# A gated attention unit feeding a long convolution: four late stores on another engine, idle products in the tail, and a plan with twenty sets of weights

## The chip, the cores and the metric

The kernel runs on one core of one Trainium2 chip. The core has a matrix engine (TensorE, PE in the profile, with PEld for its weight loads), VectorE (DVE), ScalarE (ACT), GpSimd (POOL), SyncE (SP), which here only issues transfers, and 16 DMA engines that carry all transfers. The engines run their own instruction streams in order and wait for each other on semaphores. The metric is device time in microseconds. The kernel before takes 990.45 us, the median of 3 runs (990.18 to 990.82).

## The reference

```python
def _attn_ref(u, v, z):                      # u, v: (8, 3136, 256), z: (8, 3136, 64)
    scores = (1.0 / S) * np.matmul(z, z.transpose(0, 2, 1))
    attn = np.maximum(scores, 0.0) ** 2
    out = np.matmul(attn, v)
    return (u * out).astype(np.float32)

def _moe_ref(x, w_proj, filter_fft, w_out):  # x is the output above
    proj = x @ w_proj                        # 256 -> 768
    x1, x2, x3 = proj[..., :D], proj[..., D:2 * D], proj[..., 2 * D:]
    X2 = np.fft.rfft(x2, n=S, axis=1)
    H = np.fft.rfft(filter_fft, n=S, axis=0)[None, :, :]
    x2_conv = np.fft.irfft(X2 * H, n=S, axis=1)
    y = x1 * x2_conv * x3
    return (y @ w_out).astype(np.float32)
```

There are 8 batches with a sequence of S = 3136 = 64 x 49 rows. Inputs and output are float32.

## The kernel before

**Stages of a batch.** The sequence of a batch is cut into seven chunks of columns (512, 512, 512, 512, 512, 256 and 320). For each chunk, score products (`ps_s<-zT_t`) go through ScalarE's relu (L1792) into `R_t`, are squared by VectorE (L1801) or ScalarE (L1799) into `A_t`, and are weighted with v (`ps_o_t<-A_t,v_t`). Scores are symmetric, so some blocks are turned by DMA (`M_t`, `M2e_t`, `M2o_t`) and used a second time. When a chunk's weighted sum is complete, VectorE multiplies it by u into `xT_t` (L1843); the projection products with `wp` give the two gates (`gate_t`, L1162) and the convolution's input `x_t`, which a first Fourier step (`ps_s<-x_t,T`) turns into `s_t`. That is stored to DRAM (`spec<-s_t`, L966).

When all seven chunks are stored, the batch's spectrum follows: it is loaded back in four loads (`spec_in_t<-spec`, L996; in the last batch the third and the fourth load go to `M_t` and `M2e_t`), and eight groups each take a forward product (weights `S`), two evictions, the filter's multiplication on VectorE (L1250), an inverse product (weights `TZ`), and two evictions; the results are stored to DRAM (`spec<-gs_t` and other homes, L1295) and loaded again by chunk (L1008: `conv_in_t`, and in the last batch `A_t` and `v_t`). The end of a chunk is a last Fourier step (`ps_s<-T,conv_in_t`), the gate's multiplication (`yT_t`, L1344), the output product (`wo,yT_t`), its eviction (L556 on ScalarE or L560 on VectorE, 512 columns each) and the store (`out_dram`, L1404).

**Order.** Batches overlap: one batch's projections, spectrum and chunk ends run between the scores of the next. The order is not the compiler's. A planner (class `Plan`) is run while the program is built. Each piece of work is a `Task` with a cost, dependencies and buffers; the planner keeps a clock for each engine, and picks for TensorE from the queues S (scores), Q (spectrum products), W (weighting), FA (projections and the first Fourier step), FB and FZ (other and put-off work: FZ has the last chunk ends of the batch before the last, and the last batch's gates). `pick_pe` chooses by seven numbers, a `Rule`; an eighth, `give`, is used by `pick`, which lets a copy go to ScalarE or VectorE. `rule(t)` takes the rule of the planned time t from the list `RULES`, one for each stretch of `STEP` = 50 us; in the kernel before the list has a single entry, so it holds throughout. What the planner settles is an order on each engine; the chip keeps the order and not the planned times.

**The tail.** After the last batch's last weighting nothing is left but work that depends on it: the last chunk's projection, the last store of `s_t`, the spectrum, the seven chunk ends (`add_end` with `FINAL` = (0, 2, 4, 6, 1, 3, 5) as their order), and the put-off chunk ends of the batch before, whose stores POOL issues. A chunk end's output of the last batch is stored in two halves of 64 partitions: for the chunks 0, 2, 4, 6, 1 and 3 POOL issues one half and SP the other; for chunk 5 ScalarE and SP do.

**The end.** After its last instruction each engine drains and meets the others at a barrier (L1932 in the profile), where SP also waits for the outstanding transfers.

Of the kernel before, what the change touches and what calls it, by code (L numbers as in the profile page):

```python
# [12 lines left out]
P = 128  # L13
# [17 lines left out]
LATE_F = 6.0  # L31
LATE_OUT = 1.5
LATE_POOL = 0.0
AFTER = (1, 3, 5, 6)
FINAL = (0, 2, 4, 6, 1, 3, 5)
ZP, ZL = 0, 0.0
# [1 line left out]
REACH = 2  # L38
Rule = namedtuple("Rule", "backlog ample stay first lead pace full give")
STEP = 50.0  # L40
RULES = [Rule(1.25, 5.0, 0.05, 0.5, 1, 0.5, 3.0, 1.0)]
SHARE = {0: 1, 2: 3}

ISSUED = "issued"
# [15 lines left out]
    return sum(n / 2400 + 0.003 for n in ns)  # L60


DMA_GO, DMA_DONE = {"SP": 0.3, "POOL": 2.0}, 0.9
LAT = {"PE": 0.22, "ACT": 0.22, "DVE": 0.19, "POOL": 0.15, "SP": 0.0}


# [117 lines left out]
class Plan:  # L184
# [151 lines left out]
    def pick(self, e):  # L336
# [18 lines left out]
                best = (key, s, task)  # L355
        return best and (best[1], best[2], e)

    def go(self):
        while True:
            got = []  # L360
            x = self.pick_pe()
            if x:
                got.append((x[0], 0, x[1], "PE", x[2]))
            for i, e in enumerate(self.pend):
                x = self.pick(e)
                if x:
                    got.append((x[0], i + 1, x[1], e, None))
            if not got:
                break
            start, _, task, e, k = min(got, key=lambda g: g[:2])  # L370
            if k:
                self.queues[k].remove(task)
                half = k in ("S", "Q")
                if half != (self.mode == "S") and self.mode:
                    start += 0.096
                    self.quarters, self.quad_run, self.score_run = half and self.soon, 0, 0
                self.score_run += k == "S"
                if k == "Q":
# [15 lines left out]
def kernel(  # L394
# [10 lines left out]
    nc = tc.nc  # L405
# [25 lines left out]
    plan = Plan()  # L431
# [270 lines left out]
    plan.free["POOL"] = 12.0  # L702
    plan.free["SP"] = 3.0
    plan.free["DVE"] = 1.5


    def after(task, at):
# [607 lines left out]
    def add_end(b, lasts, gtasks, cs, kind="FB", src=c_p, dsts=(o_p,), late=0, behind=(), then=(), split=False, mids=(y_p,)):  # L1315
        for at, c in enumerate(cs):
# [89 lines left out]
            if split and c == cs[-1]:  # L1406

                def both_queues(nt=nt, store=store):
                    store(0, nt, (0,))
                    store(0, nt, (1,), nc.scalar)  # L1410

                s_ = on("SP", both_queues, 0.6, [*oe, *behind], prio=1, moves=0.45 * nt)
            elif b == B - 2:
                s_ = on(
                    "POOL", lambda nt=nt, store=store: store(0, nt, by=nc.gpsimd), 1.2, [*oe, *behind],
                    moves=0.45 * nt, late=LATE_POOL,
                )
            elif split:
                s_ = on("POOL", lambda nt=nt, store=store: store(0, nt, (0,), nc.gpsimd), 0.6, [*oe, *behind], moves=0.22 * nt)
                s_ = on("SP", lambda nt=nt, store=store: store(0, nt, (1,)), 0.8, [*oe, *behind], prio=1, moves=0.22 * nt)  # L1420
            else:
                s_ = on("SP", lambda nt=nt, store=store: store(0, nt), 1.3, [*oe, *behind], prio=1, moves=0.45 * nt, late=LATE_OUT * (dst is o_p))
# [514 lines left out]
```

## Time and profile before

| | |
|---|---|
| median of 3 runs | 990.45 us |
| the profiled execution's own time | 992.91 us |
| its span, first to last instruction | 991.0 us |
| PE / DVE / ACT / POOL busy in the span | 946.0 / 831.3 / 857.8 / 207.7 us |
| granted TensorE clock, mean | 0.989 |
| DMA, mean over the span | 172 GB/s |

How to read the rows that are quoted below. A timeline row gives start, duration, engine, line, operation, output and inputs by the program's names, and a count; square brackets hold the idle time before it and what ended that. SPq, ACTq and POOLq are the sequencers of these engines, where the issue of a transfer stands. A row of the chain of waits gives start, duration and what the chain went through: an engine's line, a transfer (DMA), or "issue" where the profile shows no cause. A row of a stretch gives its bounds, then for PE, PEld, DVE, ACT and POOL the busy time and in brackets the number of instructions, then the granted clock, the mean busy share of the 16 DMA engines, and GB/s.

### The profile page before, as it was taken

The numbers are of one execution on the slowest core, as the hardware profiler recorded it, in microseconds if no ns is written. First come the engines' busy times: TensorE is split into PE (matmuls) and PEld (weight loads), VectorE is DVE, ScalarE is ACT, GpSimd is POOL, SyncE is SP. The second block draws the span as 40 slices with busy tenths as digits, with TensorE's granted clock in tenths as the row PEclk, the third lists the DMA queues.
The fourth block names the chain that finished last, engine by engine and source line by source line (L and its number), as shares of the span: only waits on it lengthen the run. The fifth ranks groups of instructions, "written<-read, shape, count | busy, mean of one in ns | idle before, by whom it ended". The sixth has DMA issues, their size and how long they took to land.

```text
span 991.0 us, 19581 instructions
## 1 busy us (share of the span) xinstructions
PE 946.0 (95%) x6774; PEld 471.2 (48%) x6878; DVE 831.3 (84%) x1461; ACT 857.8 (87%) x1192; POOL 207.7 (21%) x430
## 2 busy tenths in 40 slices
PE   6999999999999999999999999999999999999984
PEld 2344544455544545445454444445454455544643
DVE  7966798999798887988789887898879988799874
ACT  5988888899888997899988989799988899998673
POOL 5142311212021312113111320122202230001031
PEclk9999999999999999999999999999999999999978
DMA  9799879979899679997799788997889968985676
GB/s 159 144 174 168 134 151 169 177 131 168 190 206 179 127 150 220 195 174 149 148 219 200 152 137 161 218 200 136 162 171 220 193 126 175 186 219 108 167 214 199
DMA packets 332355, 170.32 MB, mean 172 GB/s; under 512 B 242582, under 2 KB 307926, under 8 KB 332256
## 3 DMA queue, kind: packets, MB, share of 16 engines
q1 hardware_dynamic: 302720, 132.82, 63.3%
q0 software_dynamic: 29456, 36.12, 23.6%
q8 instruction: 54, 0.88, 0.4%
q14 instruction: 45, 0.37, 0.1%
q10 hardware_dynamic: 80, 0.13, 0.0%
HBM read 90.26 MB, written 53.35 MB: 145 GB/s over the span
## 4 chain that ended last, share of the span: by engine, by line
PE 77%; DVE 7%; issue 6%; ACT 4%; DMA 4%; SPq 1%; POOL 1%; POOLq 0%; ACTq 0%; DVEq 0%
PE ps_o_t L523 44%; PE ps_s L523 32%; DVE A_t L1801 4%; ACT R_t L1792 3%; DVE xT_t L1843 1%; DMA uT_t<-un_t 1%; DMA spec<-s_t 1%; DMA ost_t<-in_z_dram 1%; DMA M_t<-spec 1%; ACT s_t L556 1%; SPq L996 0%; DMA specf<-s_t 0%; DVE gs_t L560 0%; ACT gs_t L556 0%; DVE xh L1250 0%
## 5 line engine op out<-in xcount | busy, mean ns | idle before, releaser
L1792 ACT ACTIVATE R_t<-ps_s 128x1024 f32<-128x1024 f32 (+4 forms) x512 | 467.5, 963 | 83.0 <-PE ps_s L523 79.3
L523 PE MATMUL ps_o_t<-A_t,v_t 128*128 128x512 bf16 (+4 forms) x2006 | 447.2, 353 | 11.9 <-issue 5.2
L1801 DVE TENSOR_TENSOR A_t<-R_t 128x1024 bf16<-128x1024 f32 (+2 forms) x324 | 354.1, 1112 | 55.5 <-ACT R_t L1792 55.0
L523 PEld LDWEIGHTS <-v_t 128*128 128x128 bf16 (+1 forms) x2884 | 248.9, 98 | 260.6 <-issue 81.4
L1799 ACT ACTIVATE A_t<-R_t 128x1024 bf16<-128x1024 f32 (+3 forms) x172 | 175.0, 1026 | 1.2
L523 PE MATMUL ps_s<-zT_t 64*64 64x512 bf16 (+4 forms) x1526 | 173.5, 358 | 1.5 <-DVE zT_t L560 0.5
L606 POOL COPY tick<-xT_t 1x1 bf16<-1x1 bf16 x54 | 19.5, 362 | 695.9 <-DVE xT_t L1843 695.9
L523 PE MATMUL ps_s<-xT_t,wp 128*128 128x512 bf16 (+2 forms) x418 | 102.8, 352 | 4.5 <-ACT R_t L1792 2.3
L523 PEld LDWEIGHTS <-zT_t 64*64 64x64 bf16 (+1 forms) x1559 | 52.1, 101 | 107.8 <-issue 93.2
L556 ACT ACTIVATE x_t<-ps_s 128x512 bf16<-128x512 f32 (+2 forms) x170 | 89.7, 583 | 11.8 <-PE ps_s L523 10.1
L1843 DVE SCALAR_TENSOR_TENSOR xT_t<-ps_o_t,uT_t 128x256 bf16<-128x256 f32 (+2 forms) x224 | 76.0, 382 | 8.7 <-PE ps_o_t L523 5.6
L523 PE MATMUL ps_o_t<-M_t,v_t 128*128 128x512 bf16 (+2 forms) x352 | 82.3, 353 | 0.1
L1250 DVE TENSOR_TENSOR xh<-xh,H 128x1024 bf16<-128x1024 bf16 x120 | 82.0, 684 | 0.2
L1162 DVE TENSOR_TENSOR gate_t<-ps_s,x_t 128x256 bf16<-128x256 f32 (+2 forms) x212 | 70.3, 383 | 14.0 <-PE ps_s L523 12.9
L1344 DVE TENSOR_TENSOR yT_t<-ps_s,gate_t 128x512 bf16<-128x512 f32 (+2 forms) x100 | 59.0, 619 | 11.1 <-PE ps_s L523 10.3
L523 PEld LDWEIGHTS <-wp 128*128 128x128 bf16 x448 | 42.9, 98 | 47.1 <-issue 11.0
L597 POOL DMA_DIRECT2D un_t<-in_u_dram x112 | 59.8, 556 | 6.4 <-issue 4.5
L616 POOL DMA_DIRECT2D v_t<-in_v_dram x112 | 59.4, 555 | 3.8 <-PE ps_s L523 1.7
L560 DVE CAST xh<-ps_s 128x512 bf16<-128x512 f32 x61 | 41.1, 688 | 22.6 <-PE ps_s L523 21.3
L523 PE MATMUL ps_s<-wp,xT_t 128*128 128x256 bf16 x396 | 56.3, 273 | 0.1
L523 PE MATMUL ps_s<-wo,yT_t 128*128 128x256 bf16 (+1 forms) x350 | 51.7, 274 | 1.7 <-DVE yT_t L1344 1.7
L556 ACT ACTIVATE s_t<-ps_s 128x512 bf16<-128x512 f32 (+1 forms) x82 | 46.8, 589 | 2.1 <-PE ps_s L523 1.1
(160 smaller groups left out, 828.4 us busy)
## 6 DMA issues: line engine op xcount, KB each, us to landing
out_dram<-ost_t SPq DMA_DIRECT2D x60, 256.0 KB
spec<-s_t SPq DMA_DIRECT2D x96, 128.0 KB
spec_in_t<-spec SPq DMA_DIRECT2D x60, 192.0 KB
spec<-gs_t SPq DMA_DIRECT2D x59, 192.0 KB
v_t<-in_v_dram POOLq DMA_DIRECT2D x80, 128.0 KB, 4.4
un_t<-in_u_dram POOLq DMA_DIRECT2D x80, 128.0 KB, 5.1
conv_in_t<-spec SPq DMA_DIRECT2D x33, 256.0 KB
out_dram<-ost_t SPq DMA_DIRECT2D x18, 128.0 KB
```

The source lines that it names most:

```text
L523: wrote(nc.tensor.matmul(o, *args, **kw), o)
L556: got = nc.scalar.activation(out_, in_, AF.Copy)
L560: got = nc.vector.tensor_copy(out_, in_)
L597: nc.gpsimd.dma_start(out=t[ds(j * N1, N1), lo - t0 : hi - t0, :], in_=x[:, n2 : n2 + hi - lo, :])
L616: nc.gpsimd.dma_start(out=t[ds(j * N1, N1), ds(v_at(a), (b - a) * D)], in_=r[:, n2 + a - lo : n2 + b - lo, :].rearrange("p t d -> p (t d)"),)
L1162: got = nc.vector.tensor_tensor(g[:, ::-1] if h == 0 else g, p, x, ALU.mult)
L1250: nc.vector.tensor_tensor(x[:, 1 - i], x[:, 0], h, ALU.mult)
L1344: got = nc.vector.tensor_tensor(yb["y"][:, dh, 0:w], p, gates[b, c, dh][:, 0:w], ALU.mult)
L1792: has_read(nc.scalar.activation(blocks(box["R"], n, cw)[:rows], p, AF.Relu), p)
L1799: nc.scalar.activation(a, r, AF.Square)
L1801: nc.vector.tensor_tensor(a, r, r, ALU.mult)
L1843: nc.vector.scalar_tensor_tensor(x, f, inv_s2, ut, ALU.mult, ALU.mult)
```

## The change

There are three parts. First, the list of rules has twenty entries. Those of the stretches from planned time 0 to 600 equal the old rule, but for one number (`pace` 0.55) in the seventh; of the eight from 600 on, four differ in `give` alone (0 in place of 1.0) and four in two to six numbers. Second, the planner gets a function `fill`: where neither scores nor weighting are left, and the next task that is picked would start at least 0.25 us (`SPARE`) after an extra product of 512 columns could have ended, such a product is put there: `ident` times a broadcast of itself, into a free bank that nobody reads. Third, in the last batch the half that POOL stored is issued by ScalarE from the third chunk in the order on (chunks 4, 6, 1 and 3); chunks 0 and 2 remain with POOL.

In the program as built, TensorE's order is the same for the first 8,155 of its 13,758 instructions (its weight loads included), and 2,502 of the rest stand in blocks that differ. 19 idle products are added, all behind the last weighting. Beside these, only the form of some products differs: among the scores of 512 columns, 20 products with weights of 64 columns are fewer and 10 with weights of 128 columns are more, since `plan.quarters` decides whether a product is issued whole or in two halves.

```diff
+SPARE = 0.25
-RULES = [Rule(1.25, 5.0, 0.05, 0.5, 1, 0.5, 3.0, 1.0)]
+RULES = [
+    Rule(1.25, 5.0, 0.05, 0.5, 1, 0.5, 3.0, 1.0),
...
+    Rule(1.25, 5.0, 0.05, 0.5, 1, 0.55, 3.0, 1.0),
...
+    Rule(1.25, 5.0, 0.05, 0.5, 1, 0.5, 3.0, 1.0),
+    Rule(1.5, 6.0, 0.15, 1, 1, 0.4, 4.0, 1.0),
+    Rule(1.25, 5.0, 0.05, 0.5, 1, 0.5, 3.0, 0),
+    Rule(2, 5.0, 0.3, 0.5, 1, 0.5, 3.0, 1.0),
+    Rule(1.25, 5.0, 0.1, 0.5, 1, 0.5, 3.5, 1.0),
+    Rule(0.75, 5.0, 0.3, 0.5, 1, 0.5, 3.5, 0.5),
+    Rule(1.25, 5.0, 0.05, 0.5, 1, 0.5, 3.0, 0),
+    Rule(1.25, 5.0, 0.05, 0.5, 1, 0.5, 3.0, 0),
+    Rule(1.25, 5.0, 0.05, 0.5, 1, 0.5, 3.0, 0),
+]
-DMA_GO, DMA_DONE = {"SP": 0.3, "POOL": 2.0}, 0.9
+DMA_GO, DMA_DONE = {"SP": 0.3, "ACT": 0.5, "POOL": 2.0}, 0.9
+    def fill(self, until):
+        if self.queues["S"] or self.queues["W"] or not any(self.queues.values()):
+            return False
+        half = 0.096 * (self.mode == "S")
+        start = self.free["PE"] + half
+        if until < start + c_pe(512) + half + SPARE or self.singles.when() > start:
+            return False
+        self.bank, self.got = self.singles, [(self.singles, self.singles.take(start))]
+        self.filler()
+        self.free["PE"] = start + c_pe(512)
+        self.singles[self.got[0][1]] = self.free["PE"]
+        self.mode, self.quarters = "W", False
+        return True
+
     def go(self):
...
             start, _, task, e, k = min(got, key=lambda g: g[:2])
+            if self.fill(start):
+                continue
...
+    plan.singles = one_slots
+    plan.filler = lambda: matmul(bank(), ident[:], ident[:].unsqueeze(1).to_broadcast([P, 4, P]), start=True, stop=True)
...
+            elif split and c in cs[:2]:
+                s_ = on("POOL", lambda nt=nt, store=store: store(0, nt, (0,), nc.gpsimd), 0.6, [*oe, *behind], moves=0.22 * nt)
+                s_ = on("SP", lambda nt=nt, store=store: store(0, nt, (1,)), 0.8, [*oe, *behind], prio=1, moves=0.22 * nt)
             elif split:
-                s_ = on("POOL", lambda nt=nt, store=store: store(0, nt, (0,), nc.gpsimd), 0.6, [*oe, *behind], moves=0.22 * nt)
+                s_ = on("ACT", lambda nt=nt, store=store: store(0, nt, (0,), nc.scalar), 0.55, [*oe, *behind], moves=0.22 * nt)
                 s_ = on("SP", lambda nt=nt, store=store: store(0, nt, (1,)), 0.8, [*oe, *behind], prio=1, moves=0.22 * nt)
```

More of the change, by code (lines that the diff above doesn't have):

```diff
@@ L40 @@
 STEP = 50.0
-RULES = [Rule(1.25, 5.0, 0.05, 0.5, 1, 0.5, 3.0, 1.0)]
+RULES = [
+    Rule(1.25, 5.0, 0.05, 0.5, 1, 0.5, 3.0, 1.0),
+    Rule(1.25, 5.0, 0.05, 0.5, 1, 0.5, 3.0, 1.0),
+    Rule(1.25, 5.0, 0.05, 0.5, 1, 0.5, 3.0, 1.0),
+    Rule(1.25, 5.0, 0.05, 0.5, 1, 0.5, 3.0, 1.0),
+    Rule(1.25, 5.0, 0.05, 0.5, 1, 0.5, 3.0, 1.0),
+    Rule(1.25, 5.0, 0.05, 0.5, 1, 0.5, 3.0, 1.0),
+    Rule(1.25, 5.0, 0.05, 0.5, 1, 0.55, 3.0, 1.0),
+    Rule(1.25, 5.0, 0.05, 0.5, 1, 0.5, 3.0, 1.0),
+    Rule(1.25, 5.0, 0.05, 0.5, 1, 0.5, 3.0, 1.0),
+    Rule(1.25, 5.0, 0.05, 0.5, 1, 0.5, 3.0, 1.0),
+    Rule(1.25, 5.0, 0.05, 0.5, 1, 0.5, 3.0, 1.0),
+    Rule(1.25, 5.0, 0.05, 0.5, 1, 0.5, 3.0, 1.0),
+    Rule(1.5, 6.0, 0.15, 1, 1, 0.4, 4.0, 1.0),
[7 more added lines that the diff above has]
+]
 SHARE = {0: 1, 2: 3}
```

## The prediction

> **What bounds the kernel now.** I read the page's shares and its clock row first, then a table of stretches, then the chain of waits through the last 60 us, then the rows at the very end.
>
> ```profile
> span 991.0 us, 19581 instructions
> PE 946.0 (95%) x6774; PEld 471.2 (48%) x6878; DVE 831.3 (84%) x1461; ACT 857.8 (87%) x1192; POOL 207.7 (21%) x430
> PEclk9999999999999999999999999999999999999978
> 604.00:932.00 328.00, 323.29 (x2365) 162.88 (x2402) 282.32 (x483) 293.04 (x406) 55.06 (x114) 1.00 0.85 175
> 936.00:963.00 27.00, 21.23 (x239) 13.09 (x239) 20.48 (x38) 19.21 (x37) 8.60 (x17) 0.75 0.76 226
> 949.00:963.00 14.00, 11.74 (x139) 6.76 (x138) 10.76 (x18) 11.33 (x22) 3.24 (x6) 0.51 0.68 208
> 973.00:981.00 8.00, 6.26 (x66) 4.94 (x64) 5.60 (x12) 5.83 (x11) 3.16 (x6) 1.00 0.79 232
> ```
>
> There are three regimes. Up to about 932 us TensorE is the bound, busy 323.3 of 328 (the last weighted product, the next fence's first row, ends at 931.7). From there PE has room: it is idle 5.8 of the 27 us from 936 to 963, though its clock is half of full from 949 on. There the chain runs through transfers:
>
> ```profile
> 931.28 0.43 PE L523 MATMUL ps_o_t<-A_t,v_t 128*128 128x320 bf16 x2
> ...
> 934.84 0.61 ACT s_t L556
> 935.46 0.36 SPq L966
> 935.92 6.06 DMA spec<-s_t
> 941.99 0.50 SPq L996
> 945.28 5.57 DMA M_t<-spec
> 950.99 2.88 PE ps_s L523 x40
> 980.08 0.55 POOLq L1932
> ```
>
> The last rows of all are not work:
>
> ```profile
> 974.71 0.52 POOL L1404 DMA_DIRECT2D out_dram<-xh  x1 [0.72 <-ACT xh L556]
> 980.10 0.53 POOL L1404 DMA_DIRECT2D out_dram<-gs_t  x1 [0.98 <-ACT gs_t L556]
> L1932 POOLq DRAIN  x3: 51/93/10108, 980.1 to 990.7; - x3
> L1932 SPq DRAIN  x3: 7/7/13, 987.1 to 990.4; - x3
> ```
>
> The last two give minimum, median and maximum in ns, and first and last start. POOL's drain starts at 980.08, with its last store, and takes 10.11, so it ends at 990.19. SP, which waits for all transfers, is at the barrier at 987.1. So the core waits for POOL 3.1 us beyond the last transfer that SP awaits. This third regime is POOL's alone.
>
> **The change part by part.** Nothing moves before the 8,155th of 13,758 PE instructions, which by a count of the trace's rows is some 604 us into it, so the rules up to there cost nothing.
>
> *1. The order from 604 us on.* With PE as the bound, a gain needs less work ahead of the last weighting, or fewer waits. Counted in the two programs, after the last weighted product stand 405 matmuls before and 444 after: 19 idle products, 16 of `T,conv_in` (four groups) and 4 of `xT,wp`. So those 20 useful ones are taken out of the full stretch.
>
> ```profile
> 930.23 0.22 PE ps_s L523 x4
> 936.72 1.03 PE L523 MATMUL ps_s<-xT_t,wp 128*128 128x512 bf16 x4
> 937.80 0.38 PE L523 MATMUL ps_o_t<-xT_t,wp 128*128 128x512 bf16 x1
> PE ps_o_t L523 <- issue: 2.1, 13, 0.2
> PE ps_s L523 <- ACT R_t L1792: 0.9, 2, 0.5
> 588.05 1.02 PE L523 MATMUL ps_o_t<-A_t,v_t 128*128 128x512 bf16 x3 [1.46 <-DVE xT_t L1843]
> L523 PE MATMUL ps_s<-zT_t 64*64 64x512 bf16 x246 | 26.8, 390 | 0.0
> L523 PE MATMUL ps_s<-zT_t 64*128 64x512 bf16 x134 | 20.2, 381 | 0.1
> ```
>
> A group of four `T,conv_in` advances the chain by 0.22: 4 x 0.22 = 0.88. A single product of 512 columns stands as 0.38, so four in 1.03 are (1.03 - 0.38) / 3 = 0.217 apart: 4 x 0.217 = 0.87. Together 1.75. The 20 half products (26.8 / 246 = 0.109 each, 2.2) that become 10 whole ones (20.2 / 134 = 0.151, 1.5) could give 0.7; I take 0.25, since overlap spreads the busy time unevenly between forms. The waits seen from 604 to 932 are 3.0 in all; I count none as won. Bounds: -5.4 (1.75 + 0.7 + 3.0) if every wait goes; +1.2 if the new order meets a wait like the one at 588 twice (2 x 1.46 - 1.75). Taken: **-2.0**. The moved work is covered by PE's 5.8 idle us, and its evictions by VectorE, idle 6.5 and ScalarE 7.8 of the same 27; without that cover its 1.75 comes back.
>
> *2. The last spectrum.* Between the last weighting and the last `x_t,T` product stand 12 `wo,yT` products before and none after, where 4 more `xT,wp` come instead. Thus the put-off chunk ends of the batch before fall behind the last Fourier step, and with them these stores:
>
> ```profile
> 935.07 2.24 POOL L1404 DMA_DIRECT2D out_dram<-ost_t  x4 [20.52 <-ACT ost_t L556]
> 936.00:942.00 6.00, 4.33 (x39) 2.99 (x38) 4.08 (x10) 2.52 (x5) 1.17 (x3) 1.00 0.88 247
> spec<-gs_t POOLq DMA_DIRECT2D x1, 192.0 KB, 2.9
> ```
>
> Four stores of 256 KB are issued around the two `spec<-s_t` puts; the engines are 0.88 busy, and the second put takes 6.06, against 2.9 for a larger one at a quieter time. So up to 3.2 of the chain could go. What is late next: the same megabyte then meets the loads of `M_t` and `M2e_t` (5.57 for one already), and VectorE and ScalarE, busy 20.5 and 19.2 of 27, have the same work. Bounds -3.2 and +1.0 (the loads wait for the whole megabyte, at 247 GB/s 4.2, less 3.2 won). Taken, nearest to the row of busy engines: **-0.8**.
>
> *3. Idle products.*
>
> ```profile
> 940.14 1.05 PE L523 MATMUL ps_s<-wo,yT_t 128*128 128x256 bf16 x8 [0.98 <-DVE yT_t L1344]
> ```
>
> 19 x 0.217 = 4.1 us of PE, 8.2 at the half clock, against 5.8 idle. They use a bank nobody waits for; those that stand where PE would wait cost nothing, and those that find their successor ready cost their time. They may hold up the clock. Held at full, the stretch from 949 could shorten only to VectorE's 10.8 or ScalarE's 11.3 of 14.0. Bounds -2.7 and +4.1; taken **0**, since the evictions of VectorE and ScalarE bound the same stretch nearly as tightly. The wait of 0.98 is the longest that a product's row shows between 932 and the drop at 949. The Trainium skill ("TensorE: Matmul & The Clock Gate", "Why this matters for your kernels") says that the clock drops after an idle gap of some 3 us. The trace disagrees, for it dropped without one. By that rule no product that fills a gap of under 1 us would matter to the clock, and the second way of the freer tail below would have no chance.
>
> *4. Four stores issued by ScalarE.*
>
> ```profile
> 979.89 0.55 ACTq L1404 DMA_DIRECT2D out_dram<-xh  x1
> L1404 SPq DMA_DIRECT2D out_dram<-xh x3: 967/1324/1918, 974.4 to 980.8; - x3
> out_dram<-gs_t POOLq DMA_DIRECT2D x2, 256.0 KB, 5.2
> 981.00:991.00 10.00, 0.00 (x0) 0.00 (x0) 0.00 (x0) 0.00 (x0) 0.00 (x0) 0.61 0.40 137
> ```
>
> One such issue takes ScalarE 0.55, so four take 2.2, and the evictions behind them wait; on a loaded queue SP needs 1.32 in the median and 1.92 at most, 5.3 and 7.7 for four. ScalarE is idle 2.2 of the 8 us from 973, and two evictions go to VectorE, idle 2.4. Behind the last issue nothing remains but transfers that the engines (0.79 busy) would still be working off. Bounds 0 and +5.5 (7.7 less 2.2 idle; 3.1 by the median). Taken **+0.4**, nearest to ScalarE's own row. SP's queue keeps its seven stores, but its last one is now 256 KB in place of 128. The moved stores also share the semaphores of SP's transfers: in the after program the two of chunk 3, the last of all, wait for those of chunk 4. Issued 4.0 earlier and 5.2 to landing (POOL's rows), these make them wait some 1 us, with nothing queued behind; that lies within the bounds.
>
> *5. POOL's drain.* POOL's last store is then the one now at 974.71, 5.4 earlier. Whether the drain is a fixed 10.1 or a wait for POOL's own transfers, it ends some 5 earlier (about 985), before SP's 987.1. The barrier then waits for SP: 990.2 - 987.1 = 3.1, less the steps between: **-3.0**. Bounds -3.0 and 0 (no other drain of such length is in the trace to tell what it waits for).
>
> Sum: -2.0 - 0.8 + 0 + 0.4 - 3.0 = -5.4. The profiled execution's own time is 992.91, so 987.5 there; against the median of the runs, which is 2.46 lower, 990.45 - 5.4 = **985.05**.
>
> **The rivals.**
>
> *The drain is not POOL's own.* If it ends a set time after the chip's last transfer (990.2 against SP's 987.1), term 5 is gone: 988.05. For it: it ends long after POOL's last issue. Against: SP, which does await everything, needs no such time. The Trainium skill ("DMA: Bandwidth & Descriptors", "Issuing engines are not separate DMA queues") says that transfers of all issuing engines run on the same 16 engines, and that another engine saves only the sequencer's time to issue. By that the move wins nothing but issue time, which is this case; the row of 0.79 busy engines agrees as far as the transfers go.
>
> *The tail runs freer.* The put lands early (-3.2 in place of -0.8) or the idle products hold the clock: 982. For it: both stand on the chain of waits. Against: VectorE and ScalarE are busy 73% there.
>
> *The order wins nothing.* The moved products find no room, or the weights bring new waits of the kind at 588: term 1 is 0, 987.05; with the drain staying too, 990.05, no change.
>
> *Idle products in the way (slower).* TensorE runs in order. In the after order runs of 4, 4 and 3 stand right ahead of spectrum products. If inputs come earlier than the plan thought and the clock is at half, 19 x 0.43 = 8.2 lies on the chain: 993.2. It decides from 7.4 on (5.4 + 2.0). For it: a row of half clock over 14 us. Against: PE's idle 5.8 in that very stretch, and each was put where the planner saw 0.25 us to spare.
>
> **How the numbers follow.** The forecast has 0.50, the drain 0.15, the freer tail 0.15, the order 0.13 (half of it with the drain staying), the idle products 0.07. A change under 0.2% (2.0 us) can't be told from none. The drain's case, 2.4 below the median, lies near that edge: I count 0.10 of it as faster and 0.05 as the same. Faster: 0.50 + 0.10 + 0.15 + 0.07 = 0.82; same: 0.05 + 0.06 = 0.11; slower: 0.07. The range leaves out the no-change and slower cases and reaches past the freer tail by half a us: 981.5 to 989.0.
>
> **What would show it.** Step 1: the last `A_t,v_t` product about 2 us earlier. Step 2: the last `spec<-s_t` landing in under 4 us, first loads right behind. Step 3: clock still at half for some windows after 945, and PE waits shorter than 0.5 ahead of spectrum products. Step 4: ACTq rows near 0.55, not 1.3, and the last eviction no later behind the first than now. Step 5: POOL's drain over before SP's. The prediction is wrong if POOL's drain still ends last, or if the put-off stores slow the loads of the spectrum by more than the put gained.

## The result and the profile after

The changed kernel takes 985.17 us in the median of six runs (983.08 to 986.41), the kernel before 990.74 beside it: a ratio of 0.9931, with a 95% interval of 0.9911 to 0.9951. A second measurement, told below, gave 0.9948 (0.9930 to 0.9967). The forecast was 985.05, a ratio of 0.9945, so both agree with it. (A ratio compares a kernel's runs with runs of the kernel before taken beside them; the quotient of the medians alone is 0.9944 in both measurements.) The sum was right, but the runs of the parts do not bear out its terms for the order and for the last spectrum.

The profiled execution took 986.41 us. Its line numbers are 38 to 43 above those of before: L561 stands for L523, L594 and L598 for the evictions of L556 and L560, L1036 for L996, L1290 for L1250, L1384 for L1344, L1444 for L1404, L1975 for L1932; each kernel of the experiments has numbers of its own. First its page: the span, TensorE's clock in 40 slices, and then the table of the four stretches that were shown of before (columns: stretch, length, busy time of PE, PEld, DVE, ACT and POOL with counts, granted clock, DMA share, GB/s).

```profile
span 984.5 us, 19596 instructions
PEclk9999999999999999999999999999999999999999
```

```profile
604.00:932.00 328.00, 323.33 (x2340) 162.84 (x2376) 279.43 (x482) 295.07 (x408) 54.13 (x114) 1.00 0.82 171
936.00:963.00 27.00, 24.49 (x277) 13.66 (x277) 23.00 (x43) 20.94 (x41) 11.23 (x21) 1.00 0.82 246
949.00:963.00 14.00, 13.11 (x145) 5.82 (x145) 12.18 (x23) 12.08 (x24) 6.86 (x13) 1.00 0.74 196
973.00:981.00 8.00, 4.09 (x42) 3.04 (x39) 4.60 (x9) 3.05 (x6) 0.05 (x1) 1.00 0.96 328
```

Two things have changed. From 949 to 963 the clock is 1.00 where it was 0.51, and VectorE is now busy 12.18 of the 14 us, ScalarE 12.08. TensorE's 13.11 hold 11 of the idle products; the chain of waits, below, runs through VectorE there. In the last stretch the DMA engines are at 0.96 where they were at 0.79, and TensorE is busy 4.1 of the 8 us where it was 6.3.

Next the timeline of the changed kernel around the last weighting and the first put-off stores (start, length, engine, line, operation), and the chain of waits through the same place:

```profile
928.26 1.79 PE L561 MATMUL ps_o_t<-A_t,v_t 128*128 128x320 bf16 x12
...
937.36 1.37 SPq L1036 DMA_DIRECT2D spec_in_t<-spec  x3
937.70 1.07 POOL L1444 DMA_DIRECT2D out_dram<-ost_t  x2 [23.89 <-ACT ost_t L594]
```

```profile
933.80 3.54 DMA spec<-s_t
...
938.24 3.59 DMA spec_in_t<-spec
941.83 0.04 issue
941.87 0.61 PE ps_s L561 x4
...
943.71 0.68 DVE xh L1290
...
958.07 0.41 DVE yT_t L1384
```

The last put of the last spectrum on SP, in the timeline of before and in that of the changed kernel:

```profile
962.80 0.77 SPq L1295 DMA_DIRECT2D spec<-uT_t  x2
960.47 0.77 SPq L1335 DMA_DIRECT2D spec<-uT_t  x2
```

The last weighted product ends at 930.05, 1.65 earlier than before. The second put takes 3.54 where it took 6.06, and the put-off stores, four of which stood around it before, now start behind it, at 937.70. In all nine kernels with the new rules it took 3.4 to 3.9, in the five with the old one 5.9 to 6.2. Its landing comes 4.6 earlier (937.34 against 941.98), but the last spectrum's put on SP only 2.3 earlier (960.47 against 962.80): between 943.7 and 958.5 the chain is almost wholly a row of VectorE's pieces. Half of the lead is given back there.

The end, on the line of the final barrier (minimum, median and maximum in ns, then first and last start), and ScalarE's issues by the timeline:

```profile
L1975 POOLq DRAIN  x3: 46/93/9271, 972.5 to 984.2; - x3
L1975 SPq DRAIN  x3: 7/7/13, 983.7 to 984.0; - x3
```

```profile
973.72 0.55 ACTq L1444 DMA_DIRECT2D out_dram<-gs_t  x1
975.03 0.67 ACTq L1444 DMA_DIRECT2D out_dram<-R_t  x1
976.37 0.78 ACTq L1444 DMA_DIRECT2D out_dram<-xh  x1
...
977.26 0.66 ACT L594 ACTIVATE xh<-ps_s 128x256 f32<-128x256 f32 x2 [0.92 <-DVE gs_t L598]
977.95 0.50 ACTq L1444 DMA_DIRECT2D out_dram<-xh  x1
978.54 0.94 ACTq L1444 DMA_DIRECT2D out_dram<-gs_t  x1
```

POOL's drain now runs from 972.51 to 981.78 and is over before SP reaches the barrier at 983.67. From there to the end of the span it is 0.8, where it was 3.9 (991.0 - 987.1).

### The profile page after: what moved, and what is told of

It is laid out like the page before. It is cut to its first block, busy times and chain, and to the rows that moved or that the text cites. A ratio compares the mean times of both kernels' runs of the same rounds, so it can differ in the third digit from the quotient of the medians.

```text
span 984.5 us, 19596 instructions
## 1 busy us (share of the span) xinstructions
PE 947.5 (96%) x6780; PEld 470.2 (48%) x6882; DVE 830.7 (84%) x1462; ACT 857.7 (87%) x1191; POOL 204.7 (21%) x426
## 4 chain that ended last, share of the span: by engine, by line
PE 78%; DVE 9%; issue 5%; ACT 4%; DMA 3%; SPq 1%; POOL 0%; DVEq 0%; ACTq 0%; POOLq 0%
PE ps_o_t L561 45%; PE ps_s L561 33%; DVE A_t L1844 4%; ACT R_t L1835 3%; DVE xT_t L1886 1%; DMA uT_t<-un_t 1%; DVE xh L1290 1%; DMA ost_t<-in_z_dram 1%; SPq L686 1%; DVE gate_t L1202 1%; DVE gs_t L598 1%; DVE R_t L1290 0%; DMA zn_t<-in_z_dram 0%; DVE yT_t L1384 0%; DMA spec_in_t<-spec 0%
## 5 line engine op out<-in xcount | busy, mean ns | idle before, releaser
L561 PE MATMUL ps_o_t<-A_t,v_t 128*128 128x512 bf16 (+4 forms) x2007 | 445.9, 353 | 11.6 <-issue 5.2
L1844 DVE TENSOR_TENSOR A_t<-R_t 128x1024 bf16<-128x1024 f32 (+3 forms) x319 | 349.8, 1115 | 60.5 <-ACT R_t L1835 59.5
L561 PEld LDWEIGHTS <-v_t 128*128 128x128 bf16 (+1 forms) x2882 | 249.0, 98 | 260.3 <-issue 79.3
L1842 ACT ACTIVATE A_t<-R_t 128x1024 bf16<-128x1024 f32 (+4 forms) x177 | 179.4, 1025 | 1.2
L561 PE MATMUL ps_s<-zT_t 64*64 64x512 bf16 (+4 forms) x1513 | 172.9, 358 | 1.5 <-DVE zT_t L598 0.5
L594 ACT ACTIVATE x_t<-ps_s 128x512 bf16<-128x512 f32 (+2 forms) x169 | 91.0, 585 | 18.1 <-PE ps_s L561 14.0
L561 PE MATMUL ps_s<-xT_t,wp 128*128 128x512 bf16 (+2 forms) x414 | 101.6, 352 | 4.1 <-ACT R_t L1835 1.8
L561 PEld LDWEIGHTS <-zT_t 64*64 64x64 bf16 (+1 forms) x1546 | 52.4, 101 | 106.2 <-issue 90.7
L1290 DVE TENSOR_TENSOR xh<-xh,H 128x1024 bf16<-128x1024 bf16 x120 | 82.2, 685 | 0.6
L561 PE MATMUL ps_o_t<-M_t,v_t 128*128 128x512 bf16 (+2 forms) x352 | 82.4, 353 | 0.0
L561 PEld LDWEIGHTS <-wp 128*128 128x128 bf16 x448 | 42.9, 98 | 45.6 <-issue 9.3
L1384 DVE TENSOR_TENSOR yT_t<-ps_s,gate_t 128x512 bf16<-128x512 f32 (+2 forms) x98 | 58.0, 623 | 6.8 <-PE ps_s L561 6.6
L598 DVE CAST xh<-ps_s 128x512 bf16<-128x512 f32 x62 | 41.8, 688 | 19.6 <-PE ps_s L561 18.0
L561 PE MATMUL ps_s<-wp,xT_t 128*128 128x256 bf16 x398 | 57.3, 273 | 0.2
L561 PE MATMUL ps_s<-wo,yT_t 128*128 128x256 bf16 (+1 forms) x342 | 51.0, 273 | 0.2
L594 ACT ACTIVATE s_t<-ps_s 128x512 bf16<-128x512 f32 (+1 forms) x81 | 46.3, 588 | 3.1 <-PE ps_s L561 1.4
```

Of the source, the lines that this page charges most:

```text
L561: wrote(nc.tensor.matmul(o, *args, **kw), o)
L594: got = nc.scalar.activation(out_, in_, AF.Copy)
L598: got = nc.vector.tensor_copy(out_, in_)
L1290: nc.vector.tensor_tensor(x[:, 1 - i], x[:, 0], h, ALU.mult)
L1384: got = nc.vector.tensor_tensor(yb["y"][:, dh, 0:w], p, gates[b, c, dh][:, 0:w], ALU.mult)
L1842: nc.scalar.activation(a, r, AF.Square)
```

## The experiments

The change has three parts: the stores (S), the rules (R) and the idle products (F). Beside the two kernels, the six other combinations of the three were made, each timed against the kernel before on its chip. Four more kernels take the drain and the put-off stores apart, one repeats the changed kernel, and one adds idle products.

### e1_stores: the stores alone

```diff
 (kernel before)
+            elif split and c in cs[:2]:
+                s_ = on("POOL", lambda nt=nt, store=store: store(0, nt, (0,), nc.gpsimd), 0.6, [*oe, *behind], moves=0.22 * nt)
+                s_ = on("SP", lambda nt=nt, store=store: store(0, nt, (1,)), 0.8, [*oe, *behind], prio=1, moves=0.22 * nt)
             elif split:
-                s_ = on("POOL", lambda nt=nt, store=store: store(0, nt, (0,), nc.gpsimd), 0.6, [*oe, *behind], moves=0.22 * nt)
+                s_ = on("ACT", lambda nt=nt, store=store: store(0, nt, (0,), nc.scalar), 0.55, [*oe, *behind], moves=0.22 * nt)
...
```

The planner's entry for an issue on ScalarE (`DMA_GO`) goes with it, as in the change.

> The kernel before, with nothing changed but the four stores of chunks 4, 6, 1 and 3, which ScalarE issues in place of POOL (old weights, no idle products). Theory D (the drain at the end is POOL's own): the barrier waits for SP, 987.1 in the profile of before, in place of POOL's 990.2, so the end comes 3.1 earlier, and the issues cost ScalarE 0 to 0.4: 987.3 to 987.8 against 990.5, a ratio of 0.9967 to 0.9972; POOL's drain ends before SP's. Rival (the drain ends a set time after the chip's last transfer): 990.4 to 991.0, ratio 1.000 to 1.0005, and POOL's drain still ends last by some 3 us. Rival (the issues hold up evictions on ScalarE): the last eviction comes 1 to 3 later and eats the gain.

Measured: 0.9955 (0.9938 to 0.9971), 4.5 us; by the medians 3.2 (988.30 against 991.50). The line of the final barrier:

```profile
L1935 POOLq DRAIN  x3: 46/93/9276, 973.9 to 987.0; - x3
L1935 SPq DRAIN  x3: 7/7/13, 986.5 to 986.8; - x3
```

POOL's drain ends at 983.22, 3.2 before SP. From the last spectrum's put (962.60) to SP's barrier it takes 23.85, where the kernel before took 23.84. ScalarE's issues took up to 1.58 here and its last eviction ended 8.91 behind the start of its first for a chunk end (before: 7.92), but SP did not arrive later for it. Theory D holds; by the ratio the part is worth more than it said (0.9967 to 0.9972), but the interval reaches that value.

### e2_fill: the idle products alone

```diff
 (kernel before)
+            if self.fill(start):
+                continue
```

The method `fill`, its spare time and its product are those of the change; the plan adds 18 products.

> The kernel before, with nothing added but idle products where the plan sees TensorE wait (18 of them; old weights, POOL keeps its stores). Theory C (the clock is what they buy): the granted clock stays at 1.0 from 949 to 963, where it was 0.51, and the last spectrum put comes 1 to 2.7 earlier: 988 to 989.5, a ratio of 0.9973 to 0.999. Theory V (VectorE and ScalarE bound that stretch all the same): the clock stays up and the put comes less than 0.5 earlier: 990.0 to 990.7, ratio 0.9995 to 1.000. Rival (idle products in the way): 991 or more. In all three POOL's drain still ends last, by some 3 us.

Measured: 0.9998 (0.9986 to 1.001). The table of stretches:

```profile
949.00:963.00 14.00, 13.27 (x155) 7.10 (x148) 11.21 (x22) 11.37 (x23) 4.86 (x9) 0.91 0.60 167
```

The clock is 0.91 in place of 0.51 (at half from 948.0 to 951.4 alone), and the time is the same. That is theory V's value, though in this profile the put comes 0.7 earlier behind the last weighting (30.8 against 31.55), where theory V allowed 0.5. POOL's drain ends at 986.83, 3.9 behind SP (982.95).

### e3_nofill: the changed kernel without idle products

```diff
 (changed kernel)
-            if self.fill(start):
-                continue
```

> The changed kernel without its 19 idle products (new weights and ScalarE's stores stay). Theory C: the clock falls to half for 10 us or more from about 945 on, and the end comes 1 to 2.7 later than the changed kernel's 985.2: 986.2 to 987.9, a ratio to before of 0.9957 to 0.9974. Theory V: the clock falls, but the end moves by less than 0.5: 985.0 to 985.7, ratio 0.9945 to 0.9952. Rival: the clock stays up without them, because the new order leaves no such gaps; then the time is that of the changed kernel.

Measured: 0.9955 (0.9938 to 0.9973), as with the stores alone. So the rules with the stores win nothing measurable over the stores, if no idle products go with them. The stretches:

```profile
949.00:963.00 14.00, 12.35 (x163) 7.19 (x166) 13.52 (x24) 11.98 (x24) 4.75 (x10) 0.74 0.68 190
```

The clock fell to half twice, from 946.0 to 949.4 and from 956.2 to 963.1. From the end of the last weighted product to POOL's part of the last spectrum's put it took 32.5 us, in the changed kernel 30.9. The ratio lies just under theory C's range (0.9957 to 0.9974), and its interval reaches the changed kernel's value.

### e4_pool: the changed kernel with the stores back on POOL

```diff
 (changed kernel)
             elif split:
-                s_ = on("ACT", lambda nt=nt, store=store: store(0, nt, (0,), nc.scalar), 0.55, [*oe, *behind], moves=0.22 * nt)
+                s_ = on("POOL", lambda nt=nt, store=store: store(0, nt, (0,), nc.gpsimd), 0.6, [*oe, *behind], moves=0.22 * nt)
```

> The changed kernel with the four stores back on POOL (new weights and idle products stay). Theory D: POOL's last store comes again at about 977.9 (the 980.1 of before less the 2.2 by which the last chunk ends came earlier), the drain ends some 10.1 later, at 988.0, and the end is 988.0 to 988.7 in the trace, against 984.5: 988.2 to 989.0 as a time, ratio 0.9977 to 0.9985. Rival (the drain is not POOL's own, the gain of 5.4 is all order and clock): 985.0 to 985.7, ratio 0.9945 to 0.9952.

Measured: 0.9985 (0.9971 to 1.0000). Three quarters of the gain are gone.

```profile
L1972 POOLq DRAIN  x3: 51/93/10383, 980.8 to 991.7; - x3
L1972 SPq DRAIN  x3: 7/7/13, 987.6 to 991.4; - x3
```

The drain ends at 991.18, 3.6 behind SP. Theory D again.

### e5_rules: the rules alone

```diff
 (kernel before)
-RULES = [Rule(1.25, 5.0, 0.05, 0.5, 1, 0.5, 3.0, 1.0)]
+RULES = [
...
+]
```

The twenty rules are those of the change.

> The kernel before with the twenty rules alone (POOL keeps its stores, no idle products). Theory O (the order's gain reaches the end): the last weighted product some 1.7 earlier against the stretch before it, the put of the spectrum under 4 us in place of 6, and the end 1.5 to 2.3 earlier: ratio 0.9977 to 0.9985. Theory G (without the full clock the gain is given back between the put and the last spectrum): the put is as short, but from the end of the last weighted product to the issue of the last spectrum's put it takes 32 to 32.5 us, where the kernel before took 31.55 and the changed kernel 30.88: ratio 0.9993 to 1.0003. In both POOL's drain ends last, 3 us or more behind SP.

Measured: 1.0007 (0.9993 to 1.0021): nothing won. The end of the last weighting by the timeline, and the first load and POOL's part of the last put by the chain:

```profile
926.88 1.79 PE L544 MATMUL ps_o_t<-A_t,v_t 128*128 128x320 bf16 x12
```

```profile
937.25 5.02 DMA spec_in_t<-spec
...
963.71 0.54 POOL spec L1316
```

The last weighted product ends at 928.67 and the last put takes 3.57, both as theory O has it; but from the end of that product to POOL's part of the last spectrum's put it takes 35.0 us, in the kernel before 31.55. That is theory G, with a larger loss than it gave. The first load landed late (5.02), and the clock was at half from 941.8 to 948.6 and from 955.5 to 962.3; the runs below take these up.

### e6_onerule: the changed kernel with the old rule

```diff
 (changed kernel)
-RULES = [
...
-]
+RULES = [Rule(1.25, 5.0, 0.05, 0.5, 1, 0.5, 3.0, 1.0)]
```

> The changed kernel with the old rule all through (ScalarE's stores and 18 idle products stay), which is the kernel before with the stores moved and idle products. Theory A (the parts add up: 0.9955 for the stores alone, 0.9998 for the idle products alone): 0.995 to 0.9958. Theory W (the idle products are worth as much here as in the changed kernel, 0.9931 against 0.9955 without them, as soon as POOL's drain no longer ends last): 0.993 to 0.9938, and the rules are worth nothing beside them. If the rules carry 1.7 to 2.3 of their own, it is 0.9948 to 0.9955 and TensorE's last weighted product comes as late as before.

Measured: 0.9963 (0.9948 to 0.9977), nearest to theory A, whose range ends at 0.9958; theory W's (0.993 to 0.9938) lies outside the interval. The clock stays whole from 827 to 984, and the stretch behind the last weighting, 29.9 us, is the shortest of all.

### e7_c3: one store alone

```diff
 (kernel before)
+            elif split and c != 3:
+                s_ = on("POOL", lambda nt=nt, store=store: store(0, nt, (0,), nc.gpsimd), 0.6, [*oe, *behind], moves=0.22 * nt)
+                s_ = on("SP", lambda nt=nt, store=store: store(0, nt, (1,)), 0.8, [*oe, *behind], prio=1, moves=0.22 * nt)
             elif split:
-                s_ = on("POOL", lambda nt=nt, store=store: store(0, nt, (0,), nc.gpsimd), 0.6, [*oe, *behind], moves=0.22 * nt)
+                s_ = on("ACT", lambda nt=nt, store=store: store(0, nt, (0,), nc.scalar), 0.55, [*oe, *behind], moves=0.22 * nt)
...
```

> The kernel before with one store moved from POOL to ScalarE, that of chunk 3, the last one POOL had. Theory L (the drain waits for POOL's own last transfer to land, and ends 4.4 to 5.1 behind it): POOL's last store is that of chunk 1, which landed at 984.2 in place of 985.6, so the drain ends some 1.5 earlier, at 988.6 to 989.3, still behind SP's 987.1: a ratio of 0.998 to 0.9988. Theory F (the drain takes a fixed 10.1 from its start, at the last issue, 978.6): it ends at 988.7 too, so the two differ by its length alone: L gives landing plus 4.4 to 5.1 whatever the length. Rival (the drain is quick once it isn't behind the last stores of all): 0.9965 to 0.997, as with all four moved.

Measured: 0.9986 (0.9974 to 0.9998), as theories L and F both have it. The barrier's line, and POOL's last store by the view of the transfers (KB each, us from issue to landing):

```profile
L1935 POOLq DRAIN  x3: 46/102/10699, 976.2 to 987.4; - x3
L1935 SPq DRAIN  x3: 7/7/13, 984.4 to 987.1; - x3
```

```profile
out_dram<-xh POOLq DMA_DIRECT2D x1, 256.0 KB, 6.2
```

That store, issued at 976.21, landed at 982.4, and the drain ended 4.5 behind it, at 986.89. It was 0.6 longer than before's because its store landed later behind its issue: theory L, not a fixed length.

### e8_nopool: none of the last stores on POOL

```diff
 (changed kernel)
-            elif split and c in cs[:2]:
-                s_ = on("POOL", lambda nt=nt, store=store: store(0, nt, (0,), nc.gpsimd), 0.6, [*oe, *behind], moves=0.22 * nt)
-                s_ = on("SP", lambda nt=nt, store=store: store(0, nt, (1,)), 0.8, [*oe, *behind], prio=1, moves=0.22 * nt)
             elif split:
```

> The changed kernel with the stores of chunks 0 and 2 on ScalarE too, so that POOL issues none of the last batch's; its last transfers are then the put-off stores, landed some 30 us before its last work. Theory L (wait for its own transfers, then some 4.4 to 5.1): the drain begins with POOL's last arithmetic and takes 5 us or less. Theory F (a fixed length): it takes 9 to 10.5. For the time: POOL's drain ended 1.9 before SP in the changed kernel, so taking more from it wins nothing; two more issues on ScalarE cost 0 to 1: ratio 0.993 to 0.994. If the changed kernel's end still hung on POOL, it would be under 0.9925.

Measured: 0.9962 (0.9944 to 0.9979), slower than expected, with runs from 983.5 to 992.2 us. The drain, and the issues ahead of it:

```profile
964.78 1.10 POOL L1444 DMA_DIRECT2D out_dram<-ost_t  x2
```

```profile
L1972 POOLq DRAIN  x3: 46/93/9239, 965.2 to 987.3; - x3
```

The last of these two landed at 968.1 (2.8 from its issue), yet the drain took 9.24. So theory L needs a floor. All fourteen profiles, of which the table has seven, fit one rule: the drain ends 9.24 to 9.28 behind its start, or 4.4 to 4.6 behind the landing of POOL's own last transfer, whichever is later. Since the drain starts with POOL's last issue in all of them, the floor may as well count from that issue.

```
kernel   drain start, length   end      own last landing   end behind it   SP at the barrier
before   980.08  10.11         990.19   985.6              4.5             987.10
e4       980.80  10.38         991.18   986.6              4.5             987.63
e7       976.19  10.70         986.89   982.4              4.5             984.43
e3       975.89  10.46         986.35   982.0              4.4             987.55
after    972.51   9.27         981.78   976.7              5.1             983.67
e1       973.94   9.28         983.22   978.3              5.0             986.45
e8       965.21   9.24         974.45   968.1              6.4             986.78
```

The time itself is lost elsewhere: from POOL's part of the last put to SP's barrier it takes 22.5 here and 22.7 in the changed kernel, so the two further issues on ScalarE are not where it goes. The timeline at the put-off stores, the group of the last spectrum's first products, and two windows of 3.4 us:

```profile
937.41 1.07 POOL L1444 DMA_DIRECT2D out_dram<-ost_t  x2 [23.89 <-ACT ost_t L594]
937.55 0.79 SPq L1036 DMA_DIRECT2D spec_in_t<-spec  x2
```

```profile
L561 PE MATMUL ps_s<-spec_in_t,S 49*64 49x512 bf16 (+1 forms) x15 | 2.1, 507 | 3.8 <-DMA spec_in_t<-spec 3.8
```

```profile
940.80:944.20 3.40, 0.00 (x0) 0.05 (x1) 0.00 (x0) 0.33 (x1) 0.98 (x2) 1.00 1.00 266
944.20:947.60 3.40, 3.34 (x26) 2.38 (x26) 1.97 (x4) 2.05 (x4) 0.00 (x0) 0.51 1.02 388
```

In the changed kernel's profile SP had issued its first load 0.34 before POOL's first put-off store. Here POOL was first, by 0.14. The third part of that load then took 5.79 from issue to landing, not 3.59, TensorE stood for 3.8 us, and the clock fell to half behind it.

### e9_again: the changed kernel again

No edit.

> The changed kernel once more, beside runs of the kernel before on this chip, since the kernel without POOL's stores came out at 0.9962 with runs spread over 9 us. If the first measurement (0.9931, 0.9911 to 0.9951) holds, the ratio is 0.992 to 0.9945. Theory R (the put-off stores and the first loads of the last spectrum race, and the changed kernel's profile showed a race that the loads had won): it is 0.9945 to 0.996, the profile has POOL's first put-off store no later than SP's first load, the third part of that load lands 2 us later behind the put than the 4.5 seen, and the clock may fall to half behind it.

Measured: 0.9948 (0.9930 to 0.9967). The two intervals overlap; the two measurements give 5.2 and 6.8 us by the ratio, 5.6 each by the medians. In this profile too SP was first by 0.34, and the load took 3.47. The race did not go against the kernel here, so theory R's own sign wasn't seen in this run, though the ratio lies in its range (0.9945 to 0.996).

### e10_hold1 and e11_hold2: the put-off stores held back

```diff
 (changed kernel, function store)
+                if by is nc.gpsimd and spec_box and "t" in spec_box[0]:
+                    nc.gpsimd.tensor_copy(seen[:], spec_box.pop()["t"][0 : EVEN + 1, 0, 0:1])
```

`spec_box` holds the tile of the last spectrum's first load, in e11 that of the second; `seen` is a tile of its own.

> The changed kernel, in which POOL, ahead of the first put-off store, copies 49 elements of the first tile that the last spectrum's loads fill, and so waits until that load has landed; everything on POOL behind it waits too. Theory R: the load lands within 4.5 us of the put in every run, TensorE waits 1.2 or less for it, the clock holds, and from the last weighted product to the last spectrum's put it takes 30 to 31.5 us, where the kernel without POOL's stores took 34.5; the ratio is 0.991 to 0.9935 and the runs lie closer together. Rival M (the same megabyte then meets the loads that come next, or the wait holds up POOL's evictions): 0.9945 to 0.997. Rival N (the race decides nothing): as the changed kernel of this call, within 0.0005.

> The same with the wait on the second tile's load, two stores later: the first two put-off stores may still race the first load, and the later ones go only when the second load has landed. Theory R: between the other two, since half of what raced is held: third part of the first load 4.5 to 5.5 behind the put, ratio 0.9925 to 0.995. Rival M: 0.995 to 0.998, the later stores landing among the loads of M and M2e. Rival N: as the changed kernel of this call.

Measured: 0.9973 (0.9960 to 0.9987) for e10, 0.9950 (0.9938 to 0.9962) for e11. The chain of e10:

```profile
938.52 2.85 DMA spec_in_t<-spec
941.37 0.05 issue
941.43 0.18 POOL seen L1448
...
942.18 5.45 DMA out_dram<-ost_t
...
947.74 0.04 ACT ost_t L594
```

Without the stores the load lands in 2.85, as theory R says, and TensorE waits 0.7 for it. But the stores themselves are now late, and ScalarE, which stood 3.6 us, goes on only at 947.74, with a tile that they had still read. From the last weighted product to POOL's part of the last put it takes 32.2, where theory R had 30 to 31.5. Rival M (0.9945 to 0.997) is nearest to the ratio. With two stores let through (e11) the time is that of the changed kernel; SP was first by 0.13, and the load took 3.21, not theory R's 4.5 to 5.5. So e11 decides between no two of the theories.

### e12_keep: idle products ahead of the load

```diff
 (changed kernel, the last spectrum's first forward product)
+                for _ in range(8 if final and g == 0 else 0):
+                    matmul(ps[:, 0, :], ident[:], ident[:].unsqueeze(1).to_broadcast([P, 4, P]), start=True, stop=True)
                 forward(ps, slot(ibox["t"], 2 * g % 4), g)
```

> The changed kernel with eight more idle products, right ahead of the first product of the last spectrum, where TensorE waited 1.0 to 3.8 us for the load in the six profiles of the new order with stores not held back, and where the clock fell to half behind every wait of 1.5 or more. They take 8 x 0.217 = 1.7 us. Theory K (the lost clock is what makes some runs slow): the clock stays at 1.0 up to 975 even where the load lands late, no run has a granted clock under 0.996, the runs lie within 3 us of each other, and the ratio is 0.992 to 0.9945. Theory D (the late load is what costs, the clock only follows it): the runs spread as those of the changed kernel (983 to 989) and the products cost up to 0.7 where the load is early: ratio 0.9948 to 0.9958. Rival (they stand in the way altogether, 1.7): 0.9958 to 0.9965.

Measured: 0.9952 (0.9936 to 0.9968), theory D's value; yet the granted clock was 0.997 or more in every run, as theory K had it. The timeline and the chain:

```profile
936.81 1.67 POOL L1446 DMA_DIRECT2D out_dram<-ost_t  x3 [23.89 <-ACT ost_t L594]
937.01 1.43 SPq L1036 DMA_DIRECT2D spec_in_t<-spec  x3
...
962.60 0.55 POOL L1337 DMA_DIRECT2D spec<-uT_t  x1 [0.92 <-ACT ost_t L594]
```

```profile
937.90 5.61 DMA spec_in_t<-spec
943.51 0.04 issue
943.55 0.61 PE ps_s L561 x4
```

This is a lost race with the clock kept: POOL was first by 0.20 and the load took 5.61. From the first product (943.55) to POOL's part of the last put (962.60) it is 19.05. In the changed kernel it is 19.06 (941.87 to 960.93), and in e8, with the clock lost, 19.98 (944.26 to 964.24). So, by these three profiles, of the 3.6 us by which e8's stretch was longer than the changed kernel's (34.5 against 30.9), 2.2 is the load and 0.9 the clock; the rest lies ahead of the load. But the ratio of e12 is no better than the changed kernel's, so keeping the clock with eight more idle products gained nothing.

The race in the profiles of the new rules in which the stores were not held back (a minus: POOL was first):

```
kernel     POOL's store behind SP's load   third part of the load   last weighting to last put
after       0.34                            3.59                     30.9
e9          0.34                            3.47                     30.8
e4          0.35                            4.03                     32.3
e3         -0.02                            4.19                     32.5
e5         -0.06                            5.02                     35.0
e12        -0.20                            5.61                     33.4
e8         -0.14                            5.79                     34.5
```

With the old rule (before, e1, e2, e6, e7), where the same stores meet the put, the stretch is 29.9 to 31.9. None of the kernels made here beats the changed one. That the stores lengthen the load is shown by e10, where it took 2.85 without them; that their order by a few tenths of a us decides by how much is the pattern of these seven profiles, and no run set the order alone.

## Why the prediction came out right

**Step 5, the drain (-3.0): right, and it carries the gain.** Moving the stores is worth 4.5 us alone, 3.5 beside the idle products (0.9998 to 0.9963), 5.2 beside the rules (1.0007 to 0.9955) and 3.7 beside both (0.9985 to 0.9948; 5.4 with the first measurement of the changed kernel): 4.2 in the mean, each with some 2 us of uncertainty. With all of POOL's stores, the span ended 3.9 to 4.7 behind SP's arrival in four profiles (before, e2, e4, e5); with the four moved, 0.8. That is 3.0 to 3.8 of the 4.2, and the term's own 3.0 is within it. "Fixed or a wait for its own" turned out to be both: a floor and a wait. The rival in which the drain is not POOL's own is refuted by e1, e4 and e7. The rule cited from the Trainium skill ("DMA: Bandwidth & Descriptors", "Issuing engines are not separate DMA queues"), that another issuing engine saves the issue alone, does not hold at the end of this kernel: e1 changed the issuing engine and won 4.5 us.

**Step 4, ScalarE's issues (+0.4): the delay was there, its cost was not seen at the end.** They took 0.50 to 0.94 each in the changed kernel, up to 1.58 in e1. The first and the last eviction of the chunk ends on ScalarE, of before and then the first of the changed kernel (its last is the row at 977.26 above):

```profile
971.89 0.60 ACT L556 ACTIVATE R_t<-ps_o_t 128x512 f32<-128x512 f32 x1 [2.38 <-PE ps_o_t L523]
979.21 0.60 ACT L556 ACTIVATE gs_t<-ps_s 128x512 f32<-128x512 f32 x1
```

```profile
969.72 0.60 ACT L594 ACTIVATE R_t<-ps_o_t 128x512 f32<-128x512 f32 x1 [2.54 <-PE ps_o_t L561]
```

From the first one's start to the last one's end it takes 7.92 before and 8.20 after; 7.92 in all five kernels in which ScalarE issues at most two stores there, 8.16 to 9.00 in the nine in which it issues five or seven. So the last eviction did come later behind the first, by 0.2 to 1.1, against the sign that the prediction gave. But from POOL's part of the last spectrum's put to SP's barrier it takes 22.5 to 23.9 in those nine and 23.1 to 23.8 in the five. The bounds (0 to +5.5) were far wider than they needed to be.

**Step 1, the order (-2.0): right where it was worked out, wrong in its cover.** The time before 604 us varies by itself, though the programs are the same there. From VectorE's 145th write of `xT_t` (574.09 in the profile of before) to the end of the last weighted product, the shortest profiles of the old rule give 355.8 to 356.0 (e1, e2, e7), those of the new rules 354.1 to 354.2 (e4, e5, e8, e9, e11): some 1.7 apart, against 1.75 counted for the moved products. The other profiles are longer (357.6 and 358.9 with the old rule, 355.1 to 355.6 with the new), and the means of all lie some 2.2 apart. But "the moved work is covered by PE's 5.8 idle us" failed: behind the last weighting the new order took 30.8 to 35.0, 32.8 in the mean of the seven profiles above, the old 29.9 to 31.9, 31.0. That is 1.8 more, about the 1.75 that the prediction said would come back without the cover. The rules alone won nothing (1.0007), and nothing beside the stores (e3 and e1 both 0.9955).

**Step 2, the last spectrum (-0.8): the put as forecast, the term wrong.** The put went from 6.06 to 3.4 to 3.9. What failed is the sentence on what is late next: it had the stores meet the loads of `M_t` and `M2e_t`, and they met the first load. They start within 0.4 us of the first load, on either side of it, and where they are first by more than 0.05 that load takes 1.4 to 2.3 longer (5.02 to 5.79, against 3.47 and 3.59). So a lost race gives back between some 0.6 of what the put won (2.2 to 2.7) and all of it. Of the lead in a won race VectorE's row of work took half, as the same sentence feared: in the changed kernel's profile 4.6 at the put's landing were 2.3 at the last spectrum's put.

**Step 3, the idle products (0): the term near, its signs wrong.** It said the clock would still be at half for some windows after 945; the changed kernel had none, and neither had e9 or e6. It said that TensorE would wait less than 0.5 ahead of spectrum products; in the changed kernel it waited 1.1 for the first load. What the held clock is worth: with the old order nothing (0.2 won alone; 0.8 lost beside the stores, 0.9955 to 0.9963), with the new 0.7 to 2.4 (e3 against the two measurements of the changed kernel) and 2.2 (e5 to e4). Rules and idle products seem to pay only together; that the products which the rules move need the full clock to fit would explain it, but no run tests that. The intervals of single kernels are about 3 us wide, so this is indicated, not settled. The rule cited there from the Trainium skill, a drop behind an idle gap of some 3 us, covers e8's wait of 3.8, not e4's of 1.5 (group of the same products), behind which the clock fell too.

So the -2.8 of steps 1 and 2 came to between +0.7 and -1.5 by the ratios (R alone; R beside S and F, 0.9963 to 0.9948; it would be -3.2 with the first measurement of the changed kernel), and the stores gave 4.2 where 2.6 was set down. By the second measurement the errors cancelled, so that the sum met the time is partly luck; how large the luck is, the two measurements leave open. The rival in which the order wins nothing seems to have happened in part, hidden by stores that were worth more.

## What to carry to other kernels

Look at what the last rows of a trace wait for: here POOL, which had issued transfers, needed at least 4.4 us after its last landing and 9.24 after its last issue, while ScalarE's drain took 0.4 to 0.6 though it issued stores to the end. So let another engine issue the final ones. When a store is moved out of the way of one transfer, ask which transfer it meets next and whether the order of the two is fixed; here a few tenths of a us seem to decide it. And time the parts of a change one by one, since a right sum may stand on wrong terms.

## What the runs showed of the hardware

POOL's drain at the barrier took 9.24 us though all of POOL's transfers had landed 6.4 us before its end (e8), so it has a floor; where the last landing is late, it ends 4.4 to 4.6 behind that. No run has a POOL without transfers, so what the floor hangs on is open.

The stretches of half clock between 930 us and the last product lasted 3.41, 6.83, 10.24 or 13.65 us in the eight profiles that have any: one to four times 3.41. The Trainium skill ("TensorE: Matmul & The Clock Gate", "Part 1: The HAM clock gate") gives a free-running window of 3413 ns, and the traces agree. It also puts the drop behind an idle window; here that is not needed. The window ahead of the drop in the profile of before:

```profile
945.70:949.10 3.40, 2.15 (x35) 1.38 (x34) 3.40 (x7) 3.00 (x7) 1.96 (x4) 1.00 0.93 302
```

TensorE was busy 0.63 of it, and in the windows ahead of the other drops 0.00 to 0.63. No sharp threshold can be read: windows of 0.57 in e2 (from 934.3) and in e7 (from 935.4) passed without a drop.

Last, the first 574 us, the same program in all profiles, took from 572.9 (e2) to 577.4 us (e4). The profiles part where a transfer lands late, at places that differ: by the waits, VectorE stood 4.7 us for a load of `zn_t` ahead of 321 us in e4, and 1.7 for `uT_t` ahead of 234 in e3. Differences of 1 us between single profiles of this kernel say nothing, unless they are counted from a common mark.
